# Attention, soft mixture of experts and a two-layer network on one core: small operations dealt to other engines, a later transpose, another load order

## The chip, the core and the metric

The kernel runs on one core of a Trainium2 chip. A core has five engines that follow their own instruction streams and meet at semaphores: TensorE (PE: matrix products and transposes, into the PSUM banks), VectorE (DVE), ScalarE (ACT), GpSimd (POOL) and SyncE (SP, which here only issues DMA transfers). The metric is the device time of one execution in microseconds (us); lower is better. An execution is timed as a whole; the profile is one more execution, recorded instruction by instruction.

## The reference

Three layers, in float32, on 4 batches of 8 heads with 576 positions of 64 values:

```
scores = q k^T / 8;   kth = 32nd largest score of each row
attn   = softmax over the scores >= kth (the others weigh nothing);   x = attn v
# x: 2304 rows x 512
logits = x @ phi                        # 32 slots: 8 experts x 4
slot_input = softmax over rows(logits)^T @ x
slot_out   = relu(slot_input @ w1[e]) @ w2[e]     # per expert e: 512 -> 1024 -> 512
y = softmax over slots(logits) @ slot_out
h = y @ w_in;   g = h (h >= 1), 0 (h <= -1), (h + 1)^2 / 4 between
out = g @ w_out                         # 512 -> 2048 -> 512
```

w_in and w_out come to the kernel as 64-bit numbers (the host only views or lays out the inputs), so each is narrowed to float32 on the chip, word by word.

## The kernel before

**Attention by pairs of heads.** 16 pairs (batch, two heads) pass through a software pipeline written out by hand: the string `ORDER` lists some 170 small steps such as `S00b` or `U31c`. The loop runs over frames, and in frame n a step with letter a, b, c or d works for pair n, n-1, n-2 or n-3. A step's first letter is its function, the first digit the row block r (0 to 3 of 128 rows for each of two heads j, and a block 4 with the 64 remaining rows of both heads), the second the head or half. PE, ACT, DVE and POOL each execute their steps in exactly this order. SP's transfers are issued in the program's order.

The steps of a row block: S scores (PE), C copy to SBUF (ACT), G and L the 24 largest scores by eights (DVE), M a mask of those scores, with O counting it on ACT where POOL made it (L379), X the scores again with the masked ones pushed down (PE) or V their product with the mask (POOL, for r = 3 and 4), K eight pad values that stand for ties (L428 on ACT, L430 on DVE), Y the next eight largest (DVE), which gives the 32nd. N scales the row maximum for the exponential (L353, POOL), B scales the 32nd score (L441, POOL), P makes a penalty from it (ACT), U subtracts it (POOL, L448), E is the exponential (ACT), T the transposes (PE), Q and R their copies (ACT), A the product with v (PE), H the copy of the result (ACT). "late" steps `lD` (L532, "den", the denominators, DVE), `lN` (POOL), `lX`, `lY` (PE), `lC`, `lE` (ACT) divide and transpose x. For the last pair H scales by the reciprocal at once and `emit_xT` transposes directly behind it. Where the masks are made follows `MASK_POOL` and `BY_V`: of nine per pair, three on POOL, six on DVE.

The steps `c0` to `c6` narrow one piece of w_in per pair: Abs, Identity and Sign on ACT (L225 to L229), Max on POOL (L231), a shift on DVE (L233), Add and Multiply on POOL (L235, L237); the piece goes back to memory as cv_d. `m` steps do the logits and running sums of a batch in the last frames of its four pairs.

**Loads of weights.** `worder` is the order of 88 pieces of 512 KB: 64 of w1 and w2 (kinds 0 and 1), 8 of cv_d (kind 2), 16 of w_out (kind 4). `wload` gives each the first free buffer of the list `wfree`; a w_out piece takes only a buffer that is one whole tile, and if there is none, nothing is issued:

```
slot = next((x for x in wfree if l < 4 or len(x) == 1), None)
if slot is None:
    return
```

22 buffers are filled during the frames. Tiles that attention no longer needs follow: q and k, the conversion's, those of the scores (`ssb`), and four `half_slots` made of two tiles each; then NB = 3 whole tiles (`wB`) that exist once attention's pools are closed. Then the ring is used again in order (`ring.pop(0)`), each as its old content is consumed, beginning with A0, which holds a w1 piece of the expert layer's first products (the seventh and eighth of 64 products, 16 of the first 96 instructions).

**Expert layer and steps.** `ex_in`, `ex_relu`, `ex_turn`, `ex_out` compute the experts; between them stand the softmax over slots (`mix_...`) and `some(f, k)`, the preparation of w_out piece f: k = 0 Abs and Identity (ACT), 1 Max and shift (DVE) and an addition (POOL), 2 sign OR (DVE), 3 copy (ACT), 4 remainder (DVE). For pieces 0 to 3 it is called there. The last stage has 96 steps: `emit_h` (PE, then Relu and Square on ACT), `emit_m`, `emit_c`, `emit_d` (DVE), and three steps later `emit_o`, nine products on PE. The two `ps_m` banks are shared by the h, so each h waits until `emit_m` of the last but one has read its bank. `todo` spreads the preparation of pieces 4 to 15 over the steps; `m_rest` at step 2 makes the rest of the matrix that all the h need.

Of the kernel before, what the change touches and what calls it, by code (L numbers as in the profile page):

```python
# [19 lines left out]
P = 128  # L20
# [15 lines left out]
NR = 4  # L36
# [7 lines left out]
NTILE = NPAIR * 9  # L44
BIG = 2.0 ** 100
NEG = -1.0e30
SIGN = -2 ** 31
CW = 512
# [7 lines left out]
NB = 3  # L56
# [3 lines left out]
MASK_POOL = ((0, 1), (1, 1), (2, 1))  # L60
NTR = 1
NV = 2
ORDER = '''
X11c R3d me G30c Q31d E40d Y10c A30d G31c U00c c1b A31d P01c O21c Y11c L3c K20c H3d me N2c T40d
Q40d B1c U01c M30c S40c E00c T41d C40c X20c G40c M31c P10c R4d S00b K21c P11c X21c me U10c Q41d
C00b Y20c E01c V30c T00c K30c Q00c S01b c4b C01b G00b c2b E10c Y21c U11c A40d T01c R0c B2c c5b
L4c V31c A41d S10b Q01c C10b Y30c P20c H4d X00b K31c E11c U20c S11b C11b T10c G01b A00c Q10c lDd
lNd c6b P21c A01c N3c E20c T11c Y31c H0c R1c M40c Q11c B3c U21c S20b V40c L0b K40c G10b C20b
M00b lYd lXd lEd P30c T20c S21b lCd z4b E21c A10c Q20c C21b A11c G11b T21c M01b K00b P31c H1c
N4c U30c Y40c L1b N1b O01b S30b G20b md R2c B4c me K01b X01b Q21c E30c A20c T30c md me M10b U31c  # L70
c0a C30b md me Y00b G21b A21c S31b Y01b E31c X10b L2b Q30c M11b P40c O11b H2c K10b c3a K11b me
T31c C31b B0b N0b U40c md M20b M21b P00b
# [6 lines left out]
def kernel_body(tc, qT, kT, vP, phi, w1, w2, w_in, w_out, out, fast, flag):  # L79
# [35 lines left out]
    worder[36:36] = [(4, 0, f) for f in range(EARLY)]  # L115
    worder += [(2, 0, n) for n in range(2 * NHP)] + [(4, 0, f) for f in range(EARLY, NF)]
# [65 lines left out]
    ends_of = p_moe.tile([P, 3], F32, name="ends_of")  # L182
    nc.vector.memset(ends_of[:, 0:1], 1.0)
    nc.vector.memset(ends_of[:, 1:2], BIG)
    phi_sb = p_moe.tile([P, NHP, 4, NSLOT], F32, name="phi_sb")
    cnt_all = p_moe.tile([P, NTILE], F32, name="cnt_all")
    less_all = p_moe.tile([P, NTILE], F32, name="less_all")
    kth_all = p_moe.tile([P, NTILE], F32, name="kth_all")
    if fast:
        nc.vector.memset(cnt_all, 0.0)  # L190
        nc.vector.memset(less_all, S)
        nc.vector.memset(kth_all, 1.0)
# [15 lines left out]
    def conv_op(i, k):  # L208
        if k == 0:
            conv_st[i] = (raw.pop(i), p_cv.tile([P, 2, CW], I32, name="tr", tag="tr", bufs=NTR),  # L210
                          p_cv.tile([P, CW], BF16, name="sg", tag="sg", bufs=NTR))
        narrow(*conv_st[i], (k,))
        if k == 2 and i + 1 < NCV:
# [51 lines left out]
    width = [2] * NR + [1]  # L265
    st = {}
    x_of = {}
    xu_of = {}

# [88 lines left out]
    def op_m(u, j):  # L358
# [4 lines left out]
        t = st[u]["t0"] + j  # L363
# [10 lines left out]
    def op_o(u, j):  # L374
        if not fast:
            return
        t = st[u]["t0"] + j
# [30 lines left out]
    def op_y(u, j):  # L408
        if not fast:
            return  # L410
        if j == 0:
            st[u]["l8"] = p_small.tile([P, 2, 8], F32, name="l8", tag="l8")
# [5 lines left out]
        nc.vector.max(st[u]["l8"][:, j], src)  # L418

    def op_k(u, j):  # L420
# [3 lines left out]
        t = st[u]["t0"] + j  # L424
        pad = st[u, "w2", j][:, S:] if v else st[u]["mb"][:, S + j * PADS:S + (j + 1) * PADS]
        n = (cnt_all, less_all)[v][:, t:t + 1]
        if v or (u[1], j) in MASK_POOL:
            nc.scalar.activation(pad, ranks[:, 1 + v], AF.Identity, bias=ends_of[:, v:v + 1], scale=n)  # L428
        else:
            nc.vector.tensor_scalar(pad, ranks[:, 0], n, 0.0, op0=ALU.subtract, op1=ALU.add, accum_out=ends_of[:, 2:3])  # L430

    def kth(u):
        return st[u]["l8"][:, :, PADS - 1] if fast else st[u]["top"][:, :, TOPK - 1]

    def op_b(u):
        n, t = width[u[1]], st[u]["t0"]
        if u[1] in BY_V:
            st[u]["kb"] = kth_all[:, t:t + n]
        else:
            st[u]["kb"] = p_small.tile([P, 2], F32, name="kb", tag="kb")  # L440
        nc.gpsimd.tensor_scalar(st[u]["kb"][:, :n], kth(u)[:, :n], BIG, None, op0=ALU.mult)  # L441

    def op_p(u, j):
        pen = st[u, "pen", j] = p_work.tile([P, S], BF16, name="pen", tag="pen")
        nc.scalar.activation(pen, row(u, j), AF.Relu, bias=st[u]["kb"][:, j:j + 1], scale=-BIG)  # L445
# [4 lines left out]
    def op_e(u, j):  # L450
        nc.scalar.activation(row(u, j), row(u, j), AF.Exp, bias=st[u]["nm"][:, j:j + 1], scale=0.125)  # L451
# [53 lines left out]
    def op_h(u):  # L505
# [9 lines left out]
        if r == 0:  # L515
            x_of[pi] = (p_x.tile([P, 9, D], F32, name="xh", tag="xh", bufs=NXH), p_x.tile([P, S], F32, name="xT", tag="xT"))
# [6 lines left out]
        emit_xT(pi, [r])  # L523

    late = {}

    def op_late(pi, k):
        if pi == NPAIR - 1:
            return
        if k == "D":  # L530
            den = late["den"] = p_small.tile([P, 9], F32, name="den", tag="den", bufs=2)
            nc.vector.tensor_scalar_add(den, xu_of[pi][:, :, D], 1e-9)  # L532
            nc.vector.reciprocal(den, den)
        elif k == "N":
            xh = p_x.tile([P, 9, D], F32, name="xh", tag="xh", bufs=NXH)
# [198 lines left out]
    calls = dict(S=op_s, C=op_c, G=op_g, L=op_l, N=op_n, M=op_m, O=op_o, X=op_x, Y=op_y, K=op_k, B=op_b, P=op_p, U=op_u,  # L734
# [36 lines left out]
    def last_pair(name, pi):  # L771
# [3 lines left out]
        if k in "PU":  # L775
            u, j = (pi, r), int(name[2])
            if k == "P":
                ex = st[u, "pen", j] = p_hold.tile([P, S], F32, name="ex", tag="mb", bufs=NMB)
                nc.scalar.activation(ex, row(u, j), AF.Exp, bias=st[u]["nm"][:, j:j + 1], scale=0.125)
            else:  # L780
                nc.vector.scalar_tensor_tensor(row(u, j), row(u, j), kth(u)[:, j:j + 1], st.pop((u, "pen", j)),
# [63 lines left out]

    wb_slots = [whole(wB, f"wB{n}", 1) for n in range(NB)]
# [260 lines left out]
    for f in range(EARLY, NF):  # L1107
        for k, lag in enumerate((0, 1, 2, 2, 3)):
            todo.setdefault((2 + (f - EARLY) * 9 // 4 + lag, k), []).append(f)
    behind = []  # L1110

    def step(i):
# [8 lines left out]
        if i == 2:  # L1121
# [44 lines left out]
    some(1, 0)  # L1166
# [7 lines left out]
    some(1, 1)  # L1174
# [3 lines left out]
    some(2, 0)  # L1178
    some(1, 2)
# [4 lines left out]
    some(1, 3, 4)  # L1184
    some(2, 1)
# [3 lines left out]
    some(3, 0)  # L1189
    some(2, 2, 3)  # L1190
    ex_out(1, range(2, 4))
    mix_turn(3)
    some(2, 4)
# [87 lines left out]
```

## Time and profile before

| | us |
|---|---|
| median of 3 runs | 805.63 |
| lowest, highest | 803.58, 807.99 |
| the profiled execution | 807.38 |
| its span | 805.5 |

| engine | busy us | share of the span |
|---|---|---|
| PE (matrix products) | 758.6 | 94% |
| DVE | 649.2 | 81% |
| ACT | 644.2 | 80% |
| PE's weight loads | 549.9 | 68% |
| POOL | 456.9 | 57% |

The span is the time from the first to the last instruction. Matrix products overlap, and the end of each is modelled, so a busy PE need not be at its peak. The shares are means over stages: POOL works almost only in the first 500 us, DMA is full only from about 530 to 585 us. The mean granted clock of PE is 0.983 of full speed.

### The profile page before, as it was taken

The numbers are of one execution on the slowest core, as the hardware profiler recorded it, in microseconds if no ns is written. First come the engines' busy times: TensorE is split into PE (matmuls) and PEld (weight loads), VectorE is DVE, ScalarE is ACT, GpSimd is POOL, SyncE is SP. The second block draws the span as 40 slices with busy tenths as digits, with TensorE's granted clock in tenths as the row PEclk, the third lists the DMA queues.
The fourth block names the chain that finished last, engine by engine and source line by source line (L and its number), as shares of the span: only waits on it lengthen the run. The fifth ranks groups of instructions, "written<-read, shape, count | busy, mean of one in ns | idle before, by whom it ended". The sixth has DMA issues, their size and how long they took to land.

```text
span 805.5 us, 15892 instructions
## 1 busy us (share of the span) xinstructions
PE 758.6 (94%) x5006; PEld 549.9 (68%) x5022; DVE 649.2 (81%) x2937; ACT 644.2 (80%) x1392; POOL 456.9 (57%) x482
## 2 busy tenths in 40 slices
PE   3799999999999999999999998898899999999996
PEld 1367677686777677767677777432477788888885
DVE  3999999999999999999999995153478876666662
ACT  3699999999999999999999997244399974545542
POOL 2699999998999999899999894002022200000000
PEclk9799999999999999999999999699999999999999
DMA  7234124224213222202202126599910020101001
GB/s 233 73 106 145 59 87 143 68 82 143 85 60 144 80 70 92 79 14 92 78 18 92 43 87 192 163 386 405 409 71 1 0 81 1 39 1 40 33 8 43
DMA packets 31726, 81.51 MB, mean 101 GB/s; under 512 B 5648, under 2 KB 6544, under 8 KB 31632
## 3 DMA queue, kind: packets, MB, share of 16 engines
q1 hardware_dynamic: 31344, 79.94, 28.2%
q8 instruction: 41, 0.67, 0.3%
q14 instruction: 53, 0.43, 0.2%
q10 hardware_dynamic: 288, 0.46, 0.2%
HBM read 71.25 MB, written 8.91 MB: 100 GB/s over the span
## 4 chain that ended last, share of the span: by engine, by line
PE 57%; DVE 18%; ACT 16%; POOL 4%; DMA 3%; issue 2%; SPq 1%; ACTq 0%; POOLq 0%; DVEq 0%
PE o_ps L1091 24%; PE av_ps L500 6%; PE s_ps L281 5%; PE pt_ps L459 5%; DVE cand L305 4%; ACT pen L445 4%; DVE l L418 4%; PE x_ps L281 3%; ACT ssb L296 3%; DVE cand L310 3%; DVE top L312 2%; PE h_ps L1055 2%; PE h L924 2%; POOL ssb L448 2%; DVE den L532 2%; DMA w<-in_moe_w_dram 2%
## 5 line engine op out<-in xcount | busy, mean ns | idle before, releaser
L1091 PE MATMUL o_ps<-whl,ghl 128*128 128x512 f32 x864 | 215.9, 394 | 0.0
L448 POOL TENSOR_TENSOR ssb<-ssb,pen 128x576 f32<-128x576 f32 x141 | 182.9, 1297 | 13.8 <-ACT pen L445 9.6
L1091 PEld LDWEIGHTS o_ps<-whl,ghl 128*128 128x128 f32 x864 | 160.7, 188 | 34.5 <-DVE ghl L1075 0.3
L305 DVE MAX8 cand<-ssb 128x8 f32<-128x82 f32 (+1 forms) x1008 | 165.1, 228 | 1.9 <-ACT ssb L296 1.9
L500 PE MATMUL av_ps<-v_sb,ptb 128*128 128x65 f32 (+1 forms) x1280 | 144.1, 262 | 0.0
L500 PEld LDWEIGHTS av_ps<-v_sb,ptb 128*128 128x128 f32 (+1 forms) x1280 | 138.8, 182 | 0.3
L281 PE MATMUL s_ps<-kt,qt 64*128 64x288 f32 x512 | 98.5, 462 | 15.5 <-ACT ssb L296 11.2
L451 ACT ACTIVATE ssb<-ssb,nm 128x576 f32<-128x576 f32 x141 | 111.8, 793 | 1.3 <-POOL ssb L448 0.9
L1057 ACT ACTIVATE rg<-h_ps,half 128x384 f32<-128x384 f32 x96 | 55.7, 580 | 67.8 <-PE h_ps L1055 67.8
L459 PE MATMUL pt_ps<-ident,ssb 128*128 128x128 f32 x640 | 100.9, 280 | 2.3 <-ACT ptb L475 0.9
L296 ACT COPY ssb<-s_ps 128x576 f32<-128x576 f32 x144 | 94.3, 655 | 7.4 <-PE s_ps L281 6.2
L1042 POOL TENSOR_TENSOR tr_l<-tr_l 128x512 int32<-128x512 int32 x16 | 20.9, 1307 | 130.1 <-PE so L947 46.2
L1063 DVE SCALAR_TENSOR_TENSOR rg<-h_ps,rg 128x384 f32<-128x384 f32 x96 | 53.3, 556 | 48.3 <-ACT rg L1058 48.3
L459 PEld LDWEIGHTS pt_ps<-ident,ssb 128*128 128x128 f32 x640 | 71.9, 146 | 29.8 <-ACT ptb L478 7.1
L369 POOL TENSOR_SCALAR mb<-ssb,top 128x576 bf16<-128x576 f32 x48 | 83.2, 1733 | 3.6 <-DVE top L312 3.6
L475 ACT COPY ptb<-pt_ps 128x512 f32<-128x512 f32 x128 | 77.6, 606 | 1.2 <-PE pt_ps L459 1.2
L418 DVE MAX8 l<-x_ps 128x8 f32<-128x584 f32 x96 | 73.0, 762 | 6.0 <-PE x_ps L400 6.0
L445 ACT ACTIVATE pen<-ssb,kb 128x576 bf16<-128x576 f32 x96 | 75.6, 788 | 2.1 <-POOL kb L441 1.8
L281 PEld LDWEIGHTS s_ps<-kt,qt 64*128 64x128 f32 x512 | 41.2, 191 | 51.2 <-ACT ssb L296 27.7
L312 DVE MAX8 top<-cand 128x8 f32<-128x56 f32 x432 | 73.2, 206 | 0.1
L406 POOL TENSOR_TENSOR w<-ssb,mb 128x576 f32<-128x576 f32 x48 | 61.5, 1282 | 0.1
L1075 DVE TENSOR_TENSOR ghl<-rg,ghl 128x384 fp32r<-128x384 f32 x96 | 55.2, 575 | 6.3 <-PE h_ps L1055 0.5
(220 smaller groups left out, 1306.8 us busy)
## 6 DMA issues: line engine op xcount, KB each, us to landing
w<-in_moe_w_dram SPq DMA_DIRECT2D x52, 512.0 KB, 6.4
x<-in_moe_w_in_dram SPq DMA_DIRECT2D x16, 512.0 KB, 4.9
w<-in_moe_w_out_dram SPq DMA_DIRECT2D x16, 512.0 KB, 10.2
w<-in_moe_w_dram SPq DMA_DIRECT2D x24, 256.0 KB, 4.7
kt<-in_k_dram SPq DMA_DIRECT2D x15, 360.0 KB, 3.0
v_sb<-in_v_dram SPq DMA_DIRECT2D x16, 325.0 KB, 4.8
qt<-in_q_dram SPq DMA_DIRECT2D x15, 320.0 KB, 3.5
out_dram<-o_sb SPq DMA_DIRECT2D x17, 256.0 KB, 2.5
```

Source lines behind the costliest of these rows:

```text
L281: nc.tensor.matmul(o, q[us], k[us, c:c + o.shape[-1]], start=True, stop=True, tile_position=(j * D, 0), skip_group_check=True)
L296: nc.scalar.copy(ssb[:, 0] if u[1] == NR else ssb[:, :, hf], st.pop((u, hf))[:, :, :HS])
L305: nc.vector.max(st[u]["cand"][:, j, 8 * g:8 * g + 8], row(u, j)[:, S * g // NSEG:S * (g + 1) // NSEG])
L312: nc.vector.max(t8, cand)
L369: nc.gpsimd.tensor_scalar(kept(u, j), row(u, j), t_u, None, op0=ALU.is_ge)
L418: nc.vector.max(st[u]["l8"][:, j], src)
L445: nc.scalar.activation(pen, row(u, j), AF.Relu, bias=st[u]["kb"][:, j:j + 1], scale=-BIG)
L448: nc.gpsimd.tensor_tensor(row(u, j), row(u, j), st.pop((u, "pen", j)), op=ALU.subtract)
L451: nc.scalar.activation(row(u, j), row(u, j), AF.Exp, bias=st[u]["nm"][:, j:j + 1], scale=0.125)
L459: nc.tensor.transpose(pt[:, c, :], pr[:, c0:c0 + P], ident)
L500: nc.tensor.matmul(o, pj[:, c, sl], v_sb[:, 4 * jj + c, :], start=False, stop=(c == NR - 1), skip_group_check=True)
L1091: nc.tensor.matmul(pos[t][n], a[:, sl], w, start=(f == 0 and k == 0), stop=(f == NF - 1 and k == 2))
```

## The change

- N is dropped: B multiplies the row maximum and the 32nd score by two factors in one operation (`kn`), and E takes its bias from there. The eight values of Y go into `top`, which has 32 columns and six buffers. Only the last pair's r = 3 and 4 still make an `nm`.
- K moves from ACT to POOL wherever it was on ACT; mask M20 moves from DVE to POOL, and with it come a count O20 on ACT and K20 on POOL.
- The narrowing loses Abs and Max: a new first pass on DVE adds and subtracts a constant (`TINY`), Sign reads its result, the shift reads the 64-bit words directly. The next piece is fetched behind step 4, not step 2.
- "den" becomes an operation that also writes an accumulator that nobody reads.
- `ORDER` is another list of the same steps (without N and `c3`, with O20).
- The last pair's `emit_xT` of a row block comes in front of the next block's A.
- w_out pieces 1 to 3 are loaded behind the experts' weights and the first two of cv_d; the preparation of piece 1 stands around the first `emit_g`, pieces 2 and 3 are in `todo`, which spaces pieces by 17/8 steps (9/4 before); `m_rest` comes at step 3.
- `half_slots` has two more pairs (w2, and xh with mb), two `late_slots` of xh tiles come at attention's end; NB is 0.

```diff
-NB = 3
+NB = 0
-MASK_POOL = ((0, 1), (1, 1), (2, 1))
+MASK_POOL = ((0, 1), (1, 1), (2, 0), (2, 1))
+NTOP = 6
...
-    worder[36:36] = [(4, 0, f) for f in range(EARLY)]
-    worder += [(2, 0, n) for n in range(2 * NHP)] + [(4, 0, f) for f in range(EARLY, NF)]
+    worder.insert(36, (4, 0, 0))
+    worder += [(2, 0, n) for n in range(2)] + [(4, 0, f) for f in range(1, EARLY)]
+    worder += [(2, 0, n) for n in range(2, 2 * NHP)] + [(4, 0, f) for f in range(EARLY, NF)]
...
+    half_slots += [((p_hold, "w2", NW2),) * 2, ((p_hold, "xh", NXH), (p_hold, "mb", NMB))]
     half_slots += [((p_hold, "ptb", 4),) * 2] * 2
+    late_slots = [((p_hold, "xh", NXH),) * 2] * 2
...
             if k == 0:
-                nc.scalar.activation(tf, hf, AF.Abs)
+                nc.vector.tensor_scalar(sg, hf, TINY, TINY, op0=ALU.add, op1=ALU.subtract)
...
             elif k == 2:
-                nc.scalar.activation(sg, hf, AF.Sign)
-            elif k == 3:
-                nc.gpsimd.tensor_scalar(tf, tf, 2.0 ** -15, None, op0=ALU.max)
+                nc.scalar.activation(sg, sg, AF.Sign)
             elif k == 4:
-                nc.vector.tensor_scalar(t, t, 3, None, op0=ALU.logical_shift_left)
+                nc.vector.tensor_scalar(t, x64[:, :, 1], 3, None, op0=ALU.logical_shift_left)
...
         if v or (u[1], j) in MASK_POOL:
-            nc.scalar.activation(pad, ranks[:, 1 + v], AF.Identity, bias=ends_of[:, v:v + 1], scale=n)
+            nc.gpsimd.tensor_scalar(pad, ranks[:, 1 + v], n, (1.0, BIG)[v], op0=ALU.mult, op1=ALU.add)
...
-        nc.gpsimd.tensor_scalar(st[u]["kb"][:, :n], kth(u)[:, :n], BIG, None, op0=ALU.mult)
+        nc.gpsimd.tensor_tensor(st[u]["kn"][:, :n], st[u]["top"][:, :n, 0:TOPK:TOPK - 1], factor[:, :n], op=ALU.mult)
...
     def op_a(u, jj):
         pi, r = u
+        if pi == NPAIR - 1 and jj == 0:
+            while xT_late:
+                emit_xT(pi, [xT_late.pop(0)])
...
-        emit_xT(pi, [r])
+        xT_late.append(r)
+        while r == NR and xT_late:
+            emit_xT(pi, [xT_late.pop(0)])
...
-            nc.vector.tensor_scalar_add(den, xu_of[pi][:, :, D], 1e-9)
+            nc.vector.tensor_scalar(den, xu_of[pi][:, :, D], 1e-9, 0.0, op0=ALU.add, op1=ALU.add, accum_out=unread)
...
+    wfree.extend(late_slots)
+    wload(len(late_slots))
     wb_slots = [whole(wB, f"wB{n}", 1) for n in range(NB)]
...
-    for f in range(EARLY, NF):
+    for f in range(2, NF):
         for k, lag in enumerate((0, 1, 2, 2, 3)):
-            todo.setdefault((2 + (f - EARLY) * 9 // 4 + lag, k), []).append(f)
+            todo.setdefault(((f - 2) * 17 // 8 + lag, k), []).append(f)
...
-        if i == 2:
+        if i == 3:
             m_rest()
...
     emit_h(steps[0])
     emit_h(steps[1])
     m_first(1, range(NHP // 2, NHP))
+    some(1, 0)
     emit_g(steps[0])
+    some(1, 1)
     emit_g(steps[1])
+    some(1, 2, 3)
     emit_h(steps[2])
     emit_g(steps[2])
+    some(1, 4)
```

## Rows read from the trace of the kernel before

**Rows 1.** Busy us (and instructions) of each engine by stretch: two frames

```profile
250.11:279.48 29.37, 28.59 (x209) 20.77 (x211) 28.59 (x156) 29.14 (x65) 27.54 (x30) 1.00 0.25 89
...
309.00:339.62 30.62, 30.57 (x267) 22.73 (x267) 29.81 (x166) 30.42 (x70) 28.11 (x31) 1.00 0.20 72
```

**Rows 2.** Instructions in time, POOL, one frame: start us, us, line, operation

```profile
254.29 0.22 POOL L441 TENSOR_SCALAR kth_all<-l 128x2 f32<-128x2 f32 x1
254.59 1.28 POOL L448 TENSOR_TENSOR ssb<-ssb,pen 128x576 f32<-128x576 f32 x1
...
257.10 1.73 POOL L369 TENSOR_SCALAR mb<-ssb,top 128x576 bf16<-128x576 f32 x1
...
263.79 1.49 POOL L231 TENSOR_SCALAR tr<-tr 128x512 f32<-128x512 f32 x1
...
274.79 1.46 POOL L448 TENSOR_TENSOR ssb<-ssb,pen 128x576 f32<-128x576 f32 x1
```

**Rows 3.** Groups by line and shape: count | busy us, mean ns | idle before

```profile
L371 DVE TENSOR_SCALAR_CACHE_REDUCE mb<-ssb,top 128x576 bf16<-128x576 f32 x48 | 38.4, 799 | 0.0
...
L379 ACT ACTIVATE ones<-mb 128x576 bf16<-128x576 bf16 x48 | 32.8, 683 | 2.8 <-POOL mb L369 2.0
...
L428 ACT ACTIVATE mb<-ranks,ends_of,cnt_all 128x8 bf16<-128x8 f32 x48 | 19.5, 406 | 0.1
...
L225 ACT ACTIVATE tr<-x 128x512 f32<-128x512 f32 x16 | 10.8, 677 | 8.2 <-DMA x<-in_moe_w_in_dram 8.1
...
L379 ACT ACTIVATION_READ_ACCUMULATOR ones<-mb 128x1 f32 x48 | 9.4, 196 | 0.0
```

**Rows 4.** Two lines' instructions: duration ns min/median/max, first and last start

```profile
L532 DVE TENSOR_SCALAR den<-xu x15: 292/1249/1253, 72.7 to 485.3; 128x9 f32<-128x9 f32 x15
...
L233 DVE TENSOR_SCALAR tr<-tr x16: 407/412/1252, 14.2 to 453.7; 128x512 int32<-128x512 int32 x16
```

**Rows 5.** Instructions in time, PE, drain; [idle before, and who ended it]

```profile
488.83 0.33 PE L549 MATMUL xT_ps<-ident,xh 128*128 128x128 f32 x1 [0.51 <-ACT xh L522]
...
504.01 0.33 PE L549 MATMUL xT_ps<-ident,xh 128*128 128x128 f32 x1 [1.06 <-ACT xh L522]
...
517.98 12.29 PE L924 MATMUL h<-w,siT 128*32 128x512 f32 x96 [0.35 <-ACT siT L827]
```

**Rows 6.** Busy by stretch, as rows 1; last: granted clock, DMA share, GB/s

```profile
505.00:510.00 5.00, 4.70 (x31) 3.61 (x30) 1.02 (x4) 1.81 (x7) 0.00 (x0) 0.50 0.46 142
...
522.00:523.00 1.00, 1.00 (x16) 0.30 (x12) 0.00 (x0) 0.00 (x0) 0.00 (x0) 1.00 0.69 201
...
575.00:600.00 25.00, 24.58 (x114) 17.05 (x113) 17.93 (x36) 18.51 (x36) 3.90 (x3) 1.00 0.51 204
```

**Rows 7.** Transfers that SP issues, in time: start us, us, line, count

```profile
516.85 5.14 SPq L163 DMA_DIRECT2D w<-in_moe_w_out_dram  x4
522.09 35.58 SPq L163 DMA_DIRECT2D w<-in_moe_w_dram  x34
```

**Rows 8.** The chain that ended last, drain: start us, us, what

```profile
540.03 7.66 DMA w<-in_moe_w_dram
...
553.08 0.52 ACT whl L1047
...
554.68 0.44 DVE tr_l L1041
...
556.58 0.70 DVE tr_l L1044
...
557.34 5.89 DMA w<-in_moe_w_dram
```

**Rows 9.** Instructions in time, ACT, DVE and PE, first steps

```profile
574.24 0.58 ACT L1057 ACTIVATE rg<-h_ps,half 128x384 f32<-128x384 f32 x1 [1.78 <-PE h_ps L1055]
...
576.00 0.55 DVE L1063 SCALAR_TENSOR_TENSOR rg<-h_ps,rg 128x384 f32<-128x384 f32 x1
...
579.05 3.63 PE L992 MATMUL m_ps<-w,so 128*32 128x512 f32 x24
```

More of the change, by code (lines that the diff above doesn't have):

```diff
@@ L43 @@
 NW2 = 2
-NTILE = NPAIR * 9
 BIG = 2.0 ** 100
@@ L47 @@
 SIGN = -2 ** 31
+TINY = 1.5 * 2.0 ** 9
 CW = 512
@@ L181, in kernel_body @@
         nc.vector.memset(ranks[:, 2, k:k + 1], -BIG / (S - TOPU - 0.5 - k))
[L182 to L188 removed]
+    unread = p_moe.tile([P, 1], F32, name="unread")
+    factor = p_moe.tile([P, 2, 2], F32, name="factor")
+    nc.vector.memset(factor[:, :, 0], -0.125)
+    nc.vector.memset(factor[:, :, 1], BIG)
+    width = [2] * NR + [1]
+    phi_sb = p_moe.tile([P, NHP, 4, NSLOT], F32, name="phi_sb")
+    n_v = sum(width[r] for r in BY_V)
+    n_x = sum(width) - n_v
+    cnt_all = p_moe.tile([P, NPAIR * n_x], F32, name="cnt_all")
+    less_all = p_moe.tile([P, NPAIR * n_v], F32, name="less_all")
+    kn_all = p_moe.tile([P, NPAIR * n_v, 2], F32, name="kn_all")
     if fast:
@@ L212, in conv_op @@
         narrow(*conv_st[i], (k,))
-        if k == 2 and i + 1 < NCV:
+        if k == 4 and i + 1 < NCV:
             conv_load(i + 1)
@@ L268, in kernel_body, with at @@
     xu_of = {}
+    def at(u, j):
+        of_v = u[1] in BY_V
+        before = sum(width[r] for r in range(u[1]) if (r in BY_V) == of_v)
+        return u[0] * (n_v if of_v else n_x) + before + j
     def row(u, j):
@@ L423, in op_k @@
         v = int(u[1] in BY_V)
-        t = st[u]["t0"] + j
         pad = st[u, "w2", j][:, S:] if v else st[u]["mb"][:, S + j * PADS:S + (j + 1) * PADS]
-        n = (cnt_all, less_all)[v][:, t:t + 1]
+        n = (cnt_all, less_all)[v][:, at(u, j):at(u, j) + 1]
         if v or (u[1], j) in MASK_POOL:
-            nc.scalar.activation(pad, ranks[:, 1 + v], AF.Identity, bias=ends_of[:, v:v + 1], scale=n)
+            nc.gpsimd.tensor_scalar(pad, ranks[:, 1 + v], n, (1.0, BIG)[v], op0=ALU.mult, op1=ALU.add)
         else:
-            nc.vector.tensor_scalar(pad, ranks[:, 0], n, 0.0, op0=ALU.subtract, op1=ALU.add, accum_out=ends_of[:, 2:3])
-    def kth(u):
-        return st[u]["l8"][:, :, PADS - 1] if fast else st[u]["top"][:, :, TOPK - 1]
+            nc.vector.tensor_scalar(pad, ranks[:, 0], n, 0.0, op0=ALU.subtract, op1=ALU.add, accum_out=unread)
     def op_b(u):
-        n, t = width[u[1]], st[u]["t0"]
+        n = width[u[1]]
         if u[1] in BY_V:
-            st[u]["kb"] = kth_all[:, t:t + n]
+            st[u]["kn"] = kn_all[:, at(u, 0):at(u, n)]
         else:
-            st[u]["kb"] = p_small.tile([P, 2], F32, name="kb", tag="kb")
-        nc.gpsimd.tensor_scalar(st[u]["kb"][:, :n], kth(u)[:, :n], BIG, None, op0=ALU.mult)
+            st[u]["kn"] = p_small.tile([P, 2, 2], F32, name="kn", tag="kn")
+        nc.gpsimd.tensor_tensor(st[u]["kn"][:, :n], st[u]["top"][:, :n, 0:TOPK:TOPK - 1], factor[:, :n], op=ALU.mult)
     def op_p(u, j):
         pen = st[u, "pen", j] = p_work.tile([P, S], BF16, name="pen", tag="pen")
-        nc.scalar.activation(pen, row(u, j), AF.Relu, bias=st[u]["kb"][:, j:j + 1], scale=-BIG)
+        nc.scalar.activation(pen, row(u, j), AF.Relu, bias=st[u]["kn"][:, j, 1:2], scale=-BIG)
     def op_u(u, j):
@@ L780, in last_pair @@
             else:
-                nc.vector.scalar_tensor_tensor(row(u, j), row(u, j), kth(u)[:, j:j + 1], st.pop((u, "pen", j)),
+                nc.vector.scalar_tensor_tensor(row(u, j), row(u, j), st[u]["top"][:, j, TOPK - 1:], st.pop((u, "pen", j)),
                                                op0=ALU.is_ge, op1=ALU.mult)
@@ L1188, in kernel_body @@
     mix_turn(2)
-    some(3, 0)
-    some(2, 2, 3)
     ex_out(1, range(2, 4))
     mix_turn(3)
-    some(2, 4)
-    some(3, 1, 2, 3, 4)
     ex_out(1, range(4, 8))
```

72 lines of the change are left out of this document (33 added, 39 removed).

## The prediction

> **What bounds the kernel now.** I read the profiled execution from its page (span 805.5 of 807.38 us), then the busy time by stage, then each engine in time, then the chain of waits. The attention stage repeats one frame per head pair. The operation "den" stands once in each, 15 times from 72.7 to 485.3 us [rows 4]; fourteen frames lie between, and I count one more for the filling ahead. An ordinary one takes 29.37 us, and all four engines are nearly full in it: ACT 29.14, DVE 28.59, PE 28.59, POOL 27.54 [rows 1]. So ACT sets the pace, with 0.2 us to spare, and nothing is won unless each of the four gets shorter or stays under the new pace. Every fourth frame, which ends a batch, takes 30.62 with PE at 30.57 [rows 1]: PE's own. Behind the frames comes a drain (last pair, then the expert layer) in which PE waits twice for weights, 7.66 and 5.89 us [rows 8], and behind it a stage of 96 steps that PE fills.
>
> **Small work dealt anew, frame by frame.** ACT loses six pad fills (K, 0.41 each) and the Abs of the weight conversion (0.68), and gains one count (O20, 0.68 and 0.2 for the accumulator read that each such count has behind it) [rows 3]: 29.14 - 2.46 - 0.68 + 0.88 = 26.9. DVE loses mask M20 (0.80) [rows 3], pad K20 (small, left out), and the addition in "den", which today lasts 1.25 of which 0.29 is work [rows 4]; it gains the conversion's new first pass, which I price like the shift beside it, 0.41 [rows 4]: 28.59 - 0.80 - 0.96 + 0.41 = 27.2. PE keeps its 28.6.
>
> POOL is where the work lands. It loses the Max of the conversion (1.49) and five scalings N (0.22, as the equal sized kth row); it gains mask M20 (1.73) and seven pad fills; the five B become two-operand products of four numbers, which I leave at 0.22 [rows 2]. No row shows a pad fill on POOL. The two-column operation takes 0.22, and from its start to the next start 0.30 pass [rows 2]; so seven cost 1.5 to 2.1, and I take 0.24 each, 1.68, nearer to the row's own duration because most stand in front of a long operation. That is 27.54 - 1.49 - 1.10 + 1.73 + 1.68 = 28.36.
>
> To this comes a price that DVE and POOL set each other. "den" lasts 292 ns at least and 1249 in the median, the shift 407 at least and 1252 at most [rows 4]: both wait until POOL's running operation is over. In return the POOL subtraction that began beside the shift took 1.46 instead of 1.28 [rows 2, 4]. The new first pass is a second operation of the shift's kind, so I add 0.18: 28.54. The changed addition in "den" writes an accumulator, as the masks on DVE do, whose durations don't show this wait; I count that 0.96 as gone. With 0.3 for gaps of 0.08 behind the small operations (four of them, as behind the kth row [rows 2]) POOL needs 28.85, and the frame becomes 28.85 instead of 29.37. Bounds: below, PE's 28.6; above, pad fills at 0.30, gaps behind all five B and both DVE passes holding POOL for their full 0.41 give 27.54 - 1.49 - 1.10 + 1.73 + 2.10 + 0.40 + 0.82 = 30.0. I take 28.85 since the sum of rows gives it. Twelve frames at 0.52 and three of PE's at half of that: 7.0 us less (from 10.4 less to 9 more).
>
> The Trainium skill speaks against this part: VectorE: DVE Perf Modes, section "What auto-detection actually checks", lets a one-source operation in SBUF use both ports whatever its stride, and GPSIMD Engine Reference, section "Specifications", says that such an operation contends with GpSimd. By that rule the new pass, which reads every second word, holds POOL like the shift; if a strided read kept to one port, POOL would need 0.18 less and the whole 2.7 us less. No row here shows a strided pass of this kind.
>
> **Last pair's transposes.** Today PE transposes each row block of the last pair right behind the scaling by ACT and waits for it: 0.51 and 1.06 us are the long waits [rows 5]. Emitted in front of the next block's value product, they find the scaled rows ready. 1.6 us less. Behind the 1.06 the granted clock of 505 to 510 us is 0.50, the 1.2 GHz level [rows 6]; if PE stays fast there, 2.5 more. Bounds 0 to 4.1; I take 1.6, since other waits stand around that stretch.
>
> **Load order and buffers.** Today the loader issues four w_out pieces from 516.85, in 5.14 us, and the first of the last 28 expert pieces at 522.09; these take 35.58, 1.27 each [rows 7]. Three pieces fewer in front would be 3.8 us. But the one left (number 36) needs a whole buffer. The four new or freed buffers offered then are pairs of halves, and NB = 0 takes the whole ones away. So the piece waits for A0, which the expert layer frees after 16 of its first 96 matmuls, 517.98 + 12.29 x 16/96 = 520.0 [rows 5], and SP's queue stands behind it: the free pairs (two of them the new buffers) wait as well. The first expert piece follows at about 521.3, 0.8 earlier than now. The hole behind today's fourth piece (201 GB/s in 522 to 523 [rows 6], against 412 worked out from the 35.58) should shrink too. I take 1.5 us (0 to 3.8). PE's 13.5 us of waiting for weights [rows 8] leaves room for it.
>
> **What that moves into the steps.** The preparation of w_out pieces 1 to 3 lay in PE's waits for weights; now piece 1 stands in front of the first steps, 2 and 3 in them. On ACT the Relu and Square of the third h come behind the piece's copy, and that behind two shift passes (about 0.44 each), the second step's own work, which covers POOL's addition, and the OR (0.70) on DVE, and the copy itself (0.52) [rows 8]. Relu 0.58 and Square about the same [rows 9] follow. 0.88 + 0.70 + 0.52 + 1.1 = 3.2 after the second step's values are done, at 576.00, when DVE today starts its third clamp [rows 9]. PE's next h waits for the bank that this clamp frees, so PE idles some 3 us; the 3.63 of m_rest [rows 9], which today fill just this place, have moved a step later. ACT, busy 18.51 of 25 us there [rows 6], gets two more pieces: 0.8. I take 4.0 us more (2 to 7). As PE is the bound behind it, nothing gives this back.
>
> **Sum.** 807.38 - 7.0 - 1.6 - 1.5 + 4.0 = 801.3 for the profiled execution. It lies 1.75 above the median of the three runs, so 799.5 against 805.63.
>
> **The rivals.**
> *PE becomes the bound (793.6).* If pad fills hide behind long operations, frames fall to PE's 28.6: 12 x 0.77 + 3 x 0.4 = 10.4, and with a full clock in the last pair 4.1; less 1.5, plus 4.0: 12.0 less. For it: all of POOL's inputs come from engines that now have 1.6 us or more to spare. Against it: POOL's gaps.
> *Nothing comes of it (805).* Pad fills at 0.30 with a gap behind most B put the frame at 29.15, 3 us less; the loads gain nothing, since the blocked piece starts later by what the three save; with 1.6 less and 4.0 more the rest is 0.6 less. For it: the row with 0.30. Against it: few of the new small operations stand one behind another.
> *Slower (813): the two passes on DVE and POOL shut each other out.* Both passes of the conversion land in POOL's long operations; DVE waits up to 1.25 for each and POOL stands still for 0.41 twice. As POOL has no slack any more, the frame becomes 29.8 (the upper bound is 30.0): 15 x 0.43 = 6.5 more, less 1.6 and 1.5, plus 4.0: 7.4 more. It decides once POOL's frame exceeds 29.4. For it: "den", at 1.25 in the median. Against it: in the new order both passes stand beside POOL's small operations. The two skill pages above state the mechanism; the trace agrees for unit stride, 1252 ns against 407 [rows 4].
> That the change doesn't do what it says is possible for the buffers alone, and is in the sum.
>
> **How the numbers follow.** Forecast 0.42, PE bound 0.28, nothing 0.18, slower 0.12. The forecast's own range is 795 to 804. To 789 to 811 I count the tail of the PE case and most of the slower one; about 0.15 is left out. Within 0.5% (4 us, about what a measurement of this kernel tells from no change) lies 801.6 to 809.7. Faster: all of 0.28 and three quarters of 0.42, 0.6; slower: 0.12 and a little; same: the rest, 0.27.
>
> **What would show it.** Frames of 28.85 between two den operations, with POOL busiest, over 28.5, and ACT near 27; "den" at 0.3; seven small POOL operations of 0.22 to 0.3 per frame; no PE wait over 0.5 in front of the last pair's transposes; the w_out piece 0 issued about 3 us behind the end of attention's last weights; a gap of about 3 us between the first two step products. Wrong if frames fall to 28.6 or don't fall, if DVE's new pass lasts 1.2, or if the steps start without the gap.

## The result and the profile after

The changed kernel takes 799.86 us (median of 18 runs, 795.9 to 804.8) against 806.53 of the kernel before beside it; the ratio is 0.992, 95% interval 0.990 to 0.994. The forecast was 799.5. The total is right, but not by its terms, and that is luck: the attention stage gained three times what was forecast, and the steps lost three times as much. The stages of the profiled executions, in us (the last two columns are experiments told below):

| stage | before | after | t1 | t5 |
|---|---|---|---|---|
| start to first den | 72.7 | 65.4 | 65.0 | 65.5 |
| first to 14th den (13 frames) | 385.9 | 372.4 | 372.4 | 372.8 |
| 14th den to first expert product | 59.4 | 58.9 | 58.9 | 57.2 |
| that to first step product | 56.1 | 55.9 | 56.8 | 57.2 |
| that to the end | 231.4 | 244.9 | 232.0 | 230.5 |
| span | 805.5 | 797.5 | 785.1 | 783.2 |

**Frames.** Busy time between neighbouring dens of the changed kernel, as in [rows 1] (length, then PE, its weight loads, DVE, ACT and POOL with their instructions, the granted clock, DMA): the first is an ordinary frame, the other two end a batch and follow it.

```profile
208.75:237.34 28.59, 28.59 (x223) 21.73 (x220) 28.19 (x158) 27.80 (x60) 28.10 (x32) 1.00 0.32 104
...
265.88:294.92 29.04, 29.04 (x251) 21.97 (x249) 27.80 (x158) 28.20 (x63) 28.55 (x32) 1.00 0.30 110
294.92:323.28 28.36, 28.36 (x253) 21.24 (x253) 27.92 (x155) 28.09 (x65) 27.87 (x32) 1.00 0.18 63
```

The ordinary frame is 0.8 us shorter than in [rows 1], and all four engines are within 0.8 us of its length. PE is full in this one; in the first three frames, of the same length, it is busy for 28.0 us only. POOL's order in such a frame (start, length, operation):

```profile
240.09 0.20 POOL L440 TENSOR_TENSOR kn_all<-top,factor 128x4 f32<-128x4 f32 x1
240.24 1.28 POOL L447 TENSOR_TENSOR ssb<-ssb,pen 128x576 f32<-128x576 f32 x1
...
244.54 0.27 POOL L430 TENSOR_SCALAR w<-ranks,less_all 128x8 f32<-128x8 f32 x1
244.89 1.29 POOL L447 TENSOR_TENSOR ssb<-ssb,pen 128x576 f32<-128x576 f32 x1
246.15 0.28 POOL L430 TENSOR_SCALAR mb<-ranks,cnt_all 128x8 bf16<-128x8 f32 x1
246.38 1.16 POOL L243 TENSOR_TENSOR tr<-tr,sg 128x512 f32<-128x512 f32 x1
...
251.82 0.39 POOL L440 TENSOR_TENSOR kn<-top,factor 128x4 f32<-128x4 f32 x1
...
260.31 0.34 POOL L430 TENSOR_SCALAR w<-ranks,less_all 128x8 f32<-128x8 f32 x1
```

Four of the seven pad fills K (L430) cost 0.23 to 0.24 from their start to the next one, as priced; the three of r = 3 and 4 (`w`) cost 0.35 to 0.42, with 0.08 of idle time in front of them and 0.08 behind. B (L440) takes 0.15 to 0.17 instead of 0.22 in four of five cases, without the gap that was allowed for. So there are gaps, but at K: 0.49 us a frame, and 28.10 busy and 0.49 idle are the whole 28.59 of an ordinary frame. Two small operations are longer (0.39, 0.34): beside them DVE runs the conversion's passes, of which the groups say (shortest, median, longest in ns):

```profile
L537 DVE TENSOR_SCALAR_CACHE_REDUCE den<-xu x15: 142/150/154, 65.4 to 464.8; 128x9 f32<-128x9 f32 x15
...
L233 DVE TENSOR_SCALAR sg<-x x16: 420/659/940, 11.9 to 423.4; 128x512 bf16<-128x512 f32 x16
...
L239 DVE TENSOR_SCALAR tr<-x x16: 420/1076/1096, 12.2 to 431.3; 128x512 int32<-128x512 int32 x16
```

"den" no longer waits for POOL [rows 4]. The two strided passes, which read every second word of x, do: 420 ns at the start of the kernel, when POOL has nothing to do, up to 1.1 us later.

**The last pair.** PE's rows there, with its idle time and who ended it, ACT's rows ahead of that wait's end, and the busy time behind:

```profile
468.24 0.21 PE L250 MATMUL xT_ps<-ident,xh 64*64 64x64 f32 x1 [1.01 <-POOL xh L541]
...
472.09 0.49 PE L500 MATMUL av_ps<-v_sb,rs 128*128 128x130 f32 x2 [2.25 <-ACT xT L567]
472.42 3.44 PE L502 MATMUL av_ps<-v_sb,ptb 128*128 128x65 f32 x16
```
```profile
470.79 0.78 ACT L788 ACTIVATE ex<-ssb,nm 128x576 f32<-128x576 f32 x1 [1.84 <-POOL nm L786]
471.47 0.56 ACT L567 COPY xT<-xT_ps 128x512 f32<-128x512 f32 x1
```
```profile
470.00:476.00 6.00, 3.91 (x19) 3.91 (x20) 2.71 (x9) 2.56 (x5) 1.42 (x5) 0.71 0.35 125
476.00:482.00 6.00, 5.86 (x35) 5.07 (x35) 2.19 (x6) 3.50 (x9) 0.00 (x0) 0.72 0.47 150
```

The waits for the scaled rows [rows 5] are gone. A single, longer one has taken their place: the next value product needs the PSUM bank that ACT frees only by copying the transposes. That copy (L567) stands on ACT behind an exponential that waits 1.84 us for POOL's `nm` (L786), the scaled row maximum that only the last pair still has and that POOL now makes late. In a2 below ACT waits there as well, 1.11 us, but the product does not need that copy. Over the 6 us behind PE's wait the mean granted clock is 0.53 (0.50 is the 1.2 GHz level).

**Loads.** What SP issued (start, span of the issues, count), to be held against [rows 7]; the first expert product stands at 496.75:

```profile
500.21 0.33 SPq L167 DMA_DIRECT2D w<-in_moe_w_out_dram  x1
500.59 36.90 SPq L167 DMA_DIRECT2D w<-in_moe_w_dram  x38
537.85 2.41 SPq L167 DMA_DIRECT2D w<-cv_d  x3
```

The blocked w_out piece is issued 3.5 us behind that product, the first expert piece 3.8 behind it; before, 4.1 [rows 5, 7]. The loads are 0.3 us earlier at most: a1 and a2 below, with the same load order, issue the first expert piece 4.1 behind.

**The steps.** The first step products on PE, those of the kernel before, and then the chain of waits of the changed kernel from 618 us on:

```profile
552.63 2.49 PE L1104 MATMUL o_ps<-whl,ghl 128*128 128x512 f32 x9
554.97 0.34 PE L1068 MATMUL h_ps<-cT,m 128*128 128x384 f32 x1
559.23 0.69 PE L1068 MATMUL h_ps<-cT,m 128*128 128x384 f32 x1 [3.93 <-DVE rg L1076]
559.72 2.76 PE L1104 MATMUL o_ps<-whl,ghl 128*128 128x512 f32 x6
```
```profile
574.09 2.50 PE L1091 MATMUL o_ps<-whl,ghl 128*128 128x512 f32 x9
576.42 0.62 PE L1055 MATMUL h_ps<-cT,m 128*128 128x384 f32 x2
576.89 2.24 PE L1091 MATMUL o_ps<-whl,ghl 128*128 128x512 f32 x9
```
```profile
619.67 0.55 DVE ghl L1088
620.22 0.61 DVE whl L1062
620.83 0.04 issue
620.87 2.11 PE o_ps L1104 x8
...
624.84 0.55 DVE ghl L1088
625.39 0.61 DVE whl L1062
626.00 0.04 issue
626.05 2.12 PE o_ps L1104 x8
```

The hole between the first two step products is there, 7.1 us from start to start instead of 2.8. But in the chain there is a second loss: the remainder of a w_out piece (whl, L1062) is made in the very step that multiplies with it, so PE waits for DVE every second step, from step 22 to step 30, and two steps take 5.18 us instead of 4.52.

### The profile page after: what moved, and what is told of

The parts are those of the page before. It is cut to its first block, busy times and chain, and to the rows that moved or that the text cites. A ratio compares the mean times of both kernels' runs of the same rounds, so it can differ in the third digit from the quotient of the medians.

```text
span 797.5 us, 15939 instructions
## 1 busy us (share of the span) xinstructions
PE 754.3 (95%) x5022; PEld 550.2 (69%) x5022; DVE 636.1 (80%) x2901; ACT 621.6 (78%) x1316; POOL 467.3 (59%) x516
## 4 chain that ended last, share of the span: by engine, by line
PE 60%; DVE 19%; POOL 7%; ACT 6%; DMA 5%; issue 2%; SPq 1%; DVEq 0%; ACTq 0%; POOLq 0%
PE o_ps L1104 22%; PE av_ps L502 9%; PE s_ps L291 6%; PE pt_ps L458 6%; DVE cand L315 5%; DVE top L421 4%; DMA w<-in_moe_w_dram 3%; PE x_ps L291 3%; POOL ssb L447 3%; PE h L937 2%; DVE cand L320 2%; PE h_ps L1068 2%; DVE top L322 2%; POOL mb L374 2%; DMA w<-cv_d 1%
## 5 line engine op out<-in xcount | busy, mean ns | idle before, releaser
L1104 PE MATMUL o_ps<-whl,ghl 128*128 128x512 f32 x864 | 221.1, 400 | 2.1 <-DVE whl L1062 2.1
L1104 PEld LDWEIGHTS o_ps<-whl,ghl 128*128 128x128 f32 x864 | 163.3, 191 | 39.5 <-DVE whl L1062 3.7
L447 POOL TENSOR_TENSOR ssb<-ssb,pen 128x576 f32<-128x576 f32 x141 | 180.3, 1283 | 2.6
L374 POOL TENSOR_SCALAR mb<-ssb,top 128x576 bf16<-128x576 f32 x64 | 110.3, 1724 | 0.9 <-DVE top L322 0.9
L306 ACT COPY ssb<-s_ps 128x576 f32<-128x576 f32 x144 | 96.1, 667 | 10.9 <-PE s_ps L291 9.6
L450 ACT ACTIVATE ssb<-ssb,kn 128x576 f32<-128x576 f32 x96 | 78.6, 818 | 0.7 <-POOL ssb L447 0.6
L444 ACT ACTIVATE pen<-ssb,kn 128x576 bf16<-128x576 f32 x96 | 75.6, 812 | 1.7 <-POOL kn L440 0.9
L421 DVE MAX8 top<-x_ps 128x8 f32<-128x584 f32 x96 | 72.8, 758 | 2.3 <-PE x_ps L405 2.0
L1088 DVE TENSOR_TENSOR ghl<-rg,ghl 128x384 fp32r<-128x384 f32 x96 | 57.0, 594 | 6.8
```

Source lines behind the costliest of these rows:

```text
L306: nc.scalar.copy(ssb[:, 0] if u[1] == NR else ssb[:, :, hf], st.pop((u, hf))[:, :, :HS])
L374: nc.gpsimd.tensor_scalar(kept(u, j), row(u, j), t_u, None, op0=ALU.is_ge)
L421: nc.vector.max(st[u]["top"][:, j, TOPU:], src)
L447: nc.gpsimd.tensor_tensor(row(u, j), row(u, j), st.pop((u, "pen", j)), op=ALU.subtract)
L1104: nc.tensor.matmul(pos[t][n], a[:, sl], w, start=(f == 0 and k == 0), stop=(f == NF - 1 and k == 2))
```

## The experiments

Each stands beside the kernel before on the same chip; ratios are to it.

**t1, the tail of before under the changed frames.** The load order, buffers and preparation calls of before; frames and transposes as changed. The edit, shortened (`-` the changed kernel, `+` t1):

```
-    worder.insert(36, (4, 0, 0)) ... (4, 0, 1..3) behind (2, 0, 0..1)
+    worder[36:36] = [(4, 0, f) for f in range(EARLY)]
-NB = 0; two more half_slots; late_slots
+NB = 3
+    some(1, ...), some(2, ...), some(3, ...) in the expert layer, as before
-    todo: (f - 2) * 17 // 8 + lag from f = 2;  m_rest at step 3
+    todo: 2 + (f - 4) * 9 // 4 + lag from f = 4;  m_rest at step 2
```

> The changed kernel with the load order, the buffers and the places of the w_out preparation of the kernel before (frames and last pair's transposes as changed). Theory: the 13.5 us that the steps lose in the changed kernel (from the first step product to the end 244.9 us against 231.4) come from the preparation of w_out pieces 1 to 3 and their later load, so 799.9 - 13.5 = 786.4, and up to 1 us more if the new buffers bring anything: 786 to 788. Rival 1: only the 4.0 us of the prediction (the hole between the first two step products) belong to the preparation and the rest to the clock or to chance: about 796. Rival 2: the gain of the frames comes from work that the new tail merely moved, so that the old tail gives no gain over the changed kernel: about 800.

787.99 us, ratio 0.978 (0.975 to 0.981). The theory holds: the steps are back at 232 us, and the gain of the frames stays. Both rivals are out.

**t2, piece 1 alone.** `worder[36:36] = [(4, 0, 0), (4, 0, 1)]`, and `some(1, ...)` back in the expert layer; pieces 2 to 15 and the buffers as changed.

> The changed kernel, with w_out piece 1 loaded beside piece 0 and prepared in the expert layer as before; pieces 2 to 15 as changed. Theory: the hole between the first two step products (7.1 us against 2.8) goes with its prelude, 4.3 us, and the later pace stays: 799.9 - 4.3 = 795.6 (794 to 797). Rival: a second piece that needs a whole buffer holds up the expert weights by as much as it saves, 799 to 801. Rival: the hole also pulls down the clock and the pace of what follows, so that nearly all 13.5 us go with it: 787 to 790.

798.29, ratio 0.988 (0.984 to 0.993). In the profile the steps fall from 244.9 to 239.2, so piece 1 in front of them costs 5.7 us: the hole and what follows it, where the changed kernel has a granted clock of 0.50 to 0.56 from 559 to 565 us. That is more than the 4.3 of the theory. The end gains less, and in part the first rival is right: with two pieces waiting for whole buffers the expert weights start 4.5 us behind the first expert product instead of 3.8, and from that product to the first step it is 1.8 us longer. Another 3.2 us went in the last pair's stretch, which varies (a2).

**t3, buffers alone.** t1 with the buffers of the changed kernel (NB = 0, the new pairs of halves).

> The changed kernel with the load order and the preparation of before, but the buffers as changed (no whole tiles wB; two more pairs of halves in the drain and two behind). Differs from t1_old_tail in the buffers alone. Theory: four w_out pieces wait for four whole buffers A0 to A3, each 1 us or so behind the last, so the expert weights start 3 to 4 us later than in t1 and the end is 2 to 4 us later: 789 to 791. Rival: the new buffers make up for it or the loads have slack: within 1 us of t1, 786 to 788.

793.79, ratio 0.983 (0.979 to 0.988): 5.8 above t1. The expert weights start 6.4 us behind the first expert product (t1: 3.9), and from that product to the first step it is 60.4 us instead of 56.8. That is the theory's mechanism, with 2.4 us at the start of the loads where 3 to 4 were expected and 3.7 at the first step, inside the 2 to 4 expected. The rest of the 5.8, which is above the range, is the stretch of the last pair: 35.2 us from the last den to the first expert product against 31.95 in t1; it varies (a2).

**t4, the pace alone.** t1 with the pieces 4 to 15 spread as in the changed kernel. `m_rest` too stays at step 3, as in the changed kernel; t1 has it at step 2.

```
-            todo.setdefault((2 + (f - EARLY) * 9 // 4 + lag, k), []).append(f)
+            todo.setdefault(((f - 2) * 17 // 8 + lag, k), []).append(f)
```

> t1_old_tail with the preparation of pieces 4 to 15 spread as in the changed kernel (17/8 steps apart, from step 4, instead of 9/4 from step 2). Theory: between 615 and 640 us of the changed kernel a pair of steps takes 5.2 us instead of 4.5 as ACT is full at 17/8; that alone costs about 5 us, so t1 + 5: 791 to 793. Rival: the pace costs nothing by itself, the steps were only late since piece 1 to 3 were: within 1 us of t1.

793.22, ratio 0.983 (0.980 to 0.987): 5.2 above t1, steps 236.4 instead of 232.0. The traces put nearly all of that 4.4 at the spacing: at the h product of step 16 t4 is 0.3 us behind t1, which bounds what `m_rest` can cost, and the two-step intervals from step 22 to step 32 lose 4.0. The arithmetic of `todo` says why: piece f is first used in step 2f; its remainder is due in step (f - 2) x 17 // 8 + 3, that is one step ahead for f up to 9 and in the same step from f = 10 (step 20) on. Step 20 runs at 615.6 us in the changed kernel and shows no wait yet; the waits for whl stand at pieces 11 to 15, in steps 22 to 30. The older spacing keeps at least one step. My expectation blamed ACT, which is busy for 22.7 of 25 us there in the changed kernel; the profile of t4 corrects that: ACT has 21.2 there, about what t5 has, and the wait is for DVE:

```profile
615.47 2.13 PE L1099 MATMUL o_ps<-whl,ghl 128*128 128x512 f32 x8 [0.23 <-DVE whl L1057]
...
620.66 2.11 PE L1099 MATMUL o_ps<-whl,ghl 128*128 128x512 f32 x8 [0.23 <-DVE whl L1057]
...
625.83 2.13 PE L1099 MATMUL o_ps<-whl,ghl 128*128 128x512 f32 x8 [0.23 <-DVE whl L1057]
```
```profile
615.00:640.00 25.00, 22.90 (x94) 17.00 (x94) 19.14 (x38) 21.21 (x42) 5.20 (x4) 1.00 0.03 11
```

The same stretch of t5, the version that is told last, at a wider spacing, with PE full and ACT as busy:

```profile
615.00:640.00 25.00, 25.00 (x112) 20.39 (x111) 20.38 (x41) 21.15 (x41) 3.19 (x3) 1.00 0.17 64
```

**b1, the filling.** The kernel before, with the conversion steps of the first w_in piece behind the first pair's C20.

```
-                if frame == first == k and name[0] == "c":
+                if frame == k and name[0] == "c" and (held or k == first):
```
(`held` is emptied only behind C20.)

> The kernel before, with one edit: the conversion steps of the first w_in piece, which stand ahead of the first score copies on ACT, are put behind the third block's copy (C20) of the first pair. Theory: in the kernel before ACT waits 8.1 us for that piece's transfer with PE's second scores behind it (first den at 72.7 us; 65.4 in the changed kernel); this alone brings 7 us: 806.0 - 7 = 799. Rival: the changed kernel fills sooner since its order is denser, so this edit gives under 1 us: 805 to 806.

803.16, ratio 0.996 (0.993 to 0.999). The first den comes 4.1 us earlier, of the 7.25 that the change brings, and the total gains 2.5 instead of 7; the theory has the place right and over half of the size. This is the row of the kernel before on ACT that nobody has looked at:

```profile
11.88 0.66 ACT L225 ACTIVATE tr<-x 128x512 f32<-128x512 f32 x1 [8.12 <-DMA x<-in_moe_w_in_dram]
```

ACT stands at the conversion of a piece that is still on its way, with the first score copies behind it. In b1 the next wait is POOL's, which does the conversion ahead of the first mask:

```profile
21.11 0.58 PE L399 MATMUL x_ps<-mb,nbig 128*128 128x512 bf16 x1 [3.27 <-POOL mb L369]
```

In the changed kernel this wait is 1.8 us, and POOL's first mask starts at 16.28 instead of 19.32 in b1: POOL no longer has the 1.5 us Max, and its Multiply (1.16) stands behind the mask. These two and the rest of the 3.2 us that b1 leaves were not tried one by one.

**b2, den alone, in the kernel before.** `tensor_scalar(den, ..., 1e-9, 0.0, op0=ALU.add, op1=ALU.add, accum_out=...)` for `tensor_scalar_add`.

> The kernel before, with one edit: the addition in den writes an accumulator, so that it lasts 0.15 instead of 1.25 us. Theory 1 (the prediction's): ACT sets the frame of before with 29.14 of 29.37, DVE has 0.8 to spare, so this gives at most the 0.23 of ACT's slack, 0 to 3 us: 803 to 806. Theory 2: DVE's stalls lie in the ring of waits through which ACT and PE are paced, so that the whole microsecond comes off each frame: 806 - 13 = 793.

803.70, ratio 0.998 (0.995 to 1.000). Ordinary frames fall from 29.36 to 29.05 us, 0.31. ACT's idle time in such a frame falls from 0.2 to 0.1 and its busy time from 29.16 to 28.95: near theory 1, which allowed 0.23, and far from theory 2's microsecond.

**a1, den alone, in the changed kernel:** the plain addition again.

> The changed kernel with the plain addition in den (as before). Theory: the plain form waits for POOL's running operation, 1.0 us on DVE; with DVE at 28.2 and PE at 28.6 of a frame of 28.6, DVE becomes the bound at 29.2 and the frame grows by 0.6 to 1.0, 14 times: 808 to 814. Rival: DVE's 28.2 contain waits on the ports that shrink in turn, and the frame stays: 800 to 802.

801.12, ratio 0.994 (0.991 to 0.996), frames of 28.6 as before the edit: the rival is right. The plain form lasts 495 ns in the median here, not 1249, as in the new order less of POOL's operation is left when it starts, and DVE has those 0.35 us to spare. The microsecond that den lost is not what made the frame shorter.

**a2, the transposes alone.** `emit_xT(pi, [r])` behind the scaling again, in place of `xT_late`.

> The changed kernel with the last pair's transposes right behind the scaling again, as before. The prediction's term: they come back at 1.6 us, 799.9 + 1.6 = 801.5 (up to 804 with the clock). Rival: the two waits of the changed kernel in the same place (1.01 for POOL, 2.25 for the transposed copy by ACT) took their place and the term is nothing: 799 to 800.5, from the last den to the expert layer's first product 32 us either way.

798.01, ratio 0.989 (0.985 to 0.994). Nothing comes back: the rival holds, and the sign leans the other way. From the last den to the first expert product a2 takes 30.3 us, t5 30.2; the kernels with the late transposes and the same frames 30.8 to 35.2 (the changed one and t1 31.95, a1, t2, t3, t4), with the clock at 1.2 GHz for all or part of the 6 us behind the 2.25 us wait. In totals the intervals overlap, so a loss of 1 to 2 us is likely and not shown. Nor does the clock fall with the late transposes alone: with the old ones and the frames of before this stretch took 32.7 us in the kernel before, 31.8 in b1 and 30.3 in b2, with some us at 0.50 in the first two.

**c1, c2, c3: who sets the frame.** One line of the changed kernel left out each: `nc.gpsimd.tensor_tensor(tf, tf, sg, op=ALU.mult)` (c1), the mask products of two of the three row blocks (c2), both (c3).

> The changed kernel without the last step of the weight conversion (the multiplication with the signs, POOL, 1.15 us a frame; w_in loses its signs). Read from the intervals between dens, 28.55 to 28.59 in ordinary frames. Theory P (the prediction's): POOL sets the frame, so an ordinary frame falls by 0.3 to 0.4, down to the next engine at 28.2. Theory E: PE sets it (28.59 of 28.59 busy), so it stays within 0.1.

> The changed kernel without four of the six 512-wide mask products of a frame (the row blocks 0 and 1 of each pair, 0.43 us for two; their 32nd largest scores come out wrong). Theory E (PE sets the frame): an ordinary frame falls by 0.3 to 0.8, to where DVE, ACT and POOL are full. Theory P (POOL sets it): it stays within 0.1.

> Both leavings-out of c1_less_pool and c2_less_pe. If one of PE and POOL alone sets the frame, this gives what that one gave; if they set it in turn, more than either: 27.9 to 28.1, down to DVE and ACT at about 28.

Single runs, of which the intervals between dens are read. The three ordinary frames ahead of the first batch's end take 28.6 us in the changed kernel, 27.6, 27.9 and 27.9 in c1, 28.6 in c2: there theory P holds, with more than the 0.4 us expected. The frames that end a batch are the reverse: 29.0 to 29.4 in the changed kernel, 29.9 in c1, 28.6 in c2. Later ordinary frames of c1 take between 27.6 and 28.75. So a single frame is the wrong measure, and the busy times over a batch's four frames are the right one; the columns are those of the first fence. The kernel before, the changed kernel, c1, c2 and c3, in this order:

```profile
191.24:309.96 118.72, 116.75 (x927) 86.28 (x930) 115.91 (x630) 117.94 (x266) 109.78 (x117) 1.00 0.28 96
```
```profile
180.53:294.92 114.39, 114.04 (x929) 85.40 (x928) 112.00 (x622) 111.54 (x243) 112.44 (x125) 1.00 0.30 105
```
```profile
179.19:293.44 114.25, 114.04 (x929) 85.72 (x931) 111.88 (x622) 111.82 (x246) 107.80 (x121) 1.00 0.30 103
```
```profile
181.35:295.79 114.44, 112.15 (x917) 84.08 (x915) 112.33 (x623) 111.81 (x245) 112.49 (x125) 1.00 0.29 104
```
```profile
179.04:292.67 113.63, 111.92 (x917) 83.99 (x915) 112.02 (x622) 111.21 (x246) 107.82 (x121) 1.00 0.30 102
```

Taking 4.6 us of work from POOL gives 0.14; taking 1.9 of busy time from PE gives nothing; both give 0.76, and then DVE stands beside PE at 112. The next batch says about the same (0.31, 0.06 and 0.94). The first one, with no batch's end ahead of it, doesn't: 1.84, 0.69 and 2.45, so over all 13 frames c1 gains 2.7 us, c2 0.5 and c3 4.6. Theory P and theory E are both half right: POOL (28.6 a frame in c2, whatever the batch does) and PE (114.04 busy in c1 as in the changed kernel) bound the batch at the same level, and what bounds next is 0.2 us a frame below. In c3 no engine is busy for more than 112.02 of 113.63, so that next bound is a chain of waits or DVE; which was not tried. c3's ordinary frames (27.6 to 28.8) are near the 27.9 to 28.1 expected, its batch frames (29.3) are not.

**t5, the best version.** t1 with the transposes of before: of the change only the frames are left.

> t1_old_tail with the last pair's transposes too as before, so that of the change only the frames' new order and work remain. Theory: the transposes' term is nothing (a2 stood 1.9 below the changed kernel, within its spread), so 788 as t1, within 2. Rival (the prediction's term): 1.6 more than t1, 789.6. It is also the candidate for the best version.

786.71, ratio 0.976 (0.973 to 0.980), within 2 us of t1 as the theory has it, on the lower side. The frames' part of the change, the filling with it, is worth about 19 us; the three others together take 12 to 13 of them away again.

## Why the prediction was right in its total and wrong in its terms

**Frames, -7.0 forecast with the filling, -13.4 measured without it** (over 13 intervals; a batch's four frames take 114.4 instead of 118.7 us). POOL does become a bound (c1), but its 28.85 was 0.26 too long: POOL is busy for 28.10 instead of 28.54, since B mostly takes 0.15 instead of 0.22 and the subtraction beside the shift goes back from 1.46 to 1.28, where the sum kept the 1.46 and added 0.18 more. The gaps are there, 0.49 instead of 0.3, at K and not at B. Ordinary frames so give 0.80 instead of 0.52. The larger miss is in the frames that end a batch and those behind them: "PE's own" took a busy PE for a needed one. PE's part of the program is the same in a frame before and after, yet its busy time over four frames fell from 116.75 to 114.04; a frame of 30.5 us and the one behind it became 57.4 to 57.6 together, from 60.0 to 60.15. The rival "PE becomes the bound" was as right as the forecast: after the change both bound the batch at one level. The c runs show that for the changed kernel; which of the moved steps relieved PE was not tried.

**Filling, counted as one more frame (0.5 at most), measured -7.25.** The step that failed is "I count one more for the filling ahead". The trace of before shows the 8.1 us wait; the frames were read from the first den on, and what lies ahead of it was not looked at. b1 shows 4.1 of the 7.25; for the rest the Max and the place of the Multiply are argued only.

**DVE's passes, 0.41 each, measured 0.66 and 1.08 in the median.** They wait for POOL as the shift did before. Here the Trainium skill was right: VectorE: DVE Perf Modes, section "What auto-detection actually checks", names no stride among its conditions for a one-source pass to take both ports, and the trace agrees: 420 ns beside an idle POOL and 1076 beside a busy one for every second word. That did not make the frame longer, since DVE still had 0.4 to 0.6 us to spare; the slower rival asked for POOL to lose 0.41 twice, and it lost 0.2 and 0.1 at two small operations.

**Last pair's transposes, -1.6 forecast, none measured (a2).** The step took away two waits and did not ask which bank the next product would need, nor what stands on ACT ahead of the copy that frees it; what would be late next was left at "other waits stand around that stretch".

**Load order and buffers, -1.5 forecast, -0.3 at most measured.** The blocking at the whole buffer was right, its end was not: A0 came free 3.5 us behind the first expert product, not 2.0. The step that failed is 12.29 x 16/96, which takes the 96 products as equally long: PE's clock is granted at 0.50 for the first 3 us, and the 16th product ends 3.4 us behind the first one's start (3.6 before). t3 shows what the blocking can cost, 2.4 us in the start of the loads with four such pieces.

**Preparation in the steps, +4.0 forecast, +13.5 measured.** The hole is 4.3 us longer than before, as worked out. "As PE is the bound behind it, nothing gives this back" is the step that failed: behind it PE was no longer the bound. The sum priced pieces 2 and 3 as 0.8 of ACT's time, and the spacing by 17/8 not at all. The runs split the 13.5 so: 5.7 for piece 1 with what follows the hole (t2), 2.8 for pieces 2 and 3 in the steps with the other load order (t2 against t4), 4.4 for the spacing (t4 against t1); the other 0.6 is t1 against the kernel before. The 2.8 show as one wait and a slow step behind it:

```profile
594.78 0.44 PE L1068 MATMUL h_ps<-cT,m 128*128 128x384 f32 x1 [1.52 <-DVE rg L1076]
595.06 3.77 PE L1104 MATMUL o_ps<-whl,ghl 128*128 128x512 f32 x9
```

In t4 the wait is 0.42 and the step 2.25; ACT is as busy in both (9.67 and 9.78 of the 10 us ahead of it). That it is further behind in the changed kernel, by the two pieces' work, would explain the wait; this is argued, not tried. The 4.4 could be read from the diff by comparing two step numbers for each piece.

So the misses are -13.7 us in frames and filling, +9.5 in the steps and +2.4 in transposes and load order; they about cancel, and the profiled execution (799.70) is 1.6 below the 801.3 forecast for it. The 1.75 taken off for the median happened not to be needed, as this execution lies at its median. Nothing in the sum made it come out within 0.4 us.

## What to carry to other kernels

When work is moved later, write down for each piece the step in which it is due and the step in which it is used; where they are the same, a stage that was bound by one engine becomes bound by a chain of them. A pipeline's filling has its own limits: look at each engine's first wait before counting it as one more round. And test whether an engine that shows as full sets the pace by taking work off it, and read the interval over a whole period (here four frames): a single frame gives to one engine what the next frame gives back.

## What the hardware showed beyond that

The stretch behind a PE wait of 2.25 us ran at a mean granted clock of 0.50 to 0.72 over 6 us in all nine kernels with the late transposes, and at 1.00 where two shorter waits (0.97 and 1.1 us) stood instead (a2, t5). A short wait is no safe sign: in the kernel before the clock was 0.50 behind one of 1.06 [rows 5, 6], in b2 1.00 behind the same wait. Beside POOL's addition in the steps, DVE's cast of 384 elements took 1.23 us instead of 0.36, in the one case looked at: the wait for POOL concerns other one-source passes as well. An addition with an accumulator (150 ns) never showed it.
